# Attention in front of two expert layers: bias by sums in one small tile, ends of two sequences as 64-row products, transposes among products, weights later, products of zeros while k loads

## The chip, the core and the metric

The kernel runs on one core of one Trainium2 chip. Its engines are TensorE (PE), VectorE (DVE), ScalarE (ACT), GpSimd (POOL) and SyncE (SP, which issues every DMA of this kernel). The metric is the device time of one execution in microseconds (us); the time before is 2064.96 us, the median of three runs (2064.05 to 2070.14).

## What is computed

Three stages follow each other:

```python
# 1. attention with random features; q, k, v are (4, 8, 576, 64), omega is (128, 64)
q_s, k_s = q * scale, k * scale
def phi(x):
    h = einsum('bhsd,md->bhsm', x, omega) - sum(x * x, axis=-1) / 2
    return exp(h - max(h, axis=-1)) / sqrt(128)
kv, z = einsum('bhsm,bhsd->bhmd', phi(k_s), v), sum(phi(k_s), axis=2)
out = einsum('bhsm,bhmd->bhsd', phi(q_s), kv) / (einsum('bhsm,bhm->bhs', phi(q_s), z) + 1e-6)
# 2. eight experts on the 2304 tokens: gates by eight rounds of row and column sums,
#    out += gate[:, e] * (relu(x @ w1[e]) @ w2[e])
# 3. h = x @ w_in; g = h * sigmoid(1.702 h); g @ w_out
```

## The kernel before

Every step is recorded first. `Plan.add` takes an operation with its engine, an estimated duration and the tiles that it reads and writes; `Plan.run` then lists the operations engine by engine in the order in which a clock of its own would start them, and that order is written into the program. On the chip each engine works through its own list strictly in order and waits at the head of it for whatever that instruction needs. Operations of PE marked `main` keep the order in which they were recorded; the other engines take the operation with the earliest due time. `nb` is the earliest time at which the plan lets an operation start.

**Attention** goes by tiles of 128 tokens and 8 heads: 4 whole tiles for each of the 4 sequences, and one tile for the last 64 tokens of two sequences together (a tail). `attention()` builds a list of 36 steps (k tiles of a sequence, then its q tiles) and runs a pipeline over it. At step `s`:

- `squares` for tile `s+5`: POOL squares the tile (L529), DVE sums each head (L530) into `ss`.
- `project_in` for `s+4`: four PE transposes (L539), ACT and DVE split the result into a rounded part and a rest (L545, L548).
- `transpose_q` for a q tile `s`: eight PE transposes of its features (L642), ACT copies (L647).
- `features` for `s+2`: in two halves of four heads, six products each with omega (L566 to L568) into one PSUM bank each; DVE takes the maximum of each head (L574).
- `exps` for `s+2`: two small DVE operations on 128x8 (L590, L595) make the bias from `ss` and the maximum, then eight ACT exponentials (L602) read the two banks. The banks are six, taken in turn; a bank is free again when its reader is done.
- `kv_step` for a k tile (L615), or `attend` for a q tile (L659): eight products (each shown as two instructions) into the PSUM tile `pair`; for q, `divide` on DVE (L676, L681, L684).
- `transpose_x` for q tile `s-1`: four transposes (L698), ACT and DVE write the token block (L702, L705); after six tiles `x_operands` sums the pieces of the block on POOL (L405) and sends them to DRAM (`sx`).

For a q tail `attend` runs once with the first sequence's sums, `divide` writes 64 rows, then `attend` runs again with the other sequence's sums into the same `pair`, and `divide` writes the other 64 rows.

**The weights** of the first two products are recorded ahead of attention: `load_gate` (L470, L473) and `prepare(0, ...)` with `split`: four DMAs into `raw` for each half, four differences on POOL (L405, raw<-raw), then ACT casts (L1075) and POOL rests (L405, w1x and w2x).

**The expert layers** (`all_visits`) multiply by seven products of half blocks: L1169 up, L1314 down. `load_x` brings the seven pieces of a token block from `sx` into `xo`, seven DMAs of 768 KB, into room in which the attention stage kept omega and its split tiles. The first four products of the first visit are taken early, at the places of `EARLY` within the last steps of attention. The first product of all (L1387) only wipes a bank.

## Time and profile before

| what | value |
|---|---|
| median of three runs | 2064.96 us (2064.05 to 2070.14) |
| the profiled execution's own time, its span | 2075.01 us, 2073.2 us |
| mean granted TensorE clock in it | 0.984 of full speed |
| PE busy | 2007.5 us, 97% of the span |
| DVE, ACT, POOL busy | 1474.2 us (71%), 1080.6 us (52%), 1270.5 us (61%) |
| chain that ended last, by engine | PE 78%, DVE 13%, ACT 3%, DMA 2% |

"Busy" counts the time in which an engine has an instruction in it. PE counts as busy at either of its two clocks, 1.2 and 2.4 GHz, so a stretch in which PE is always busy can still take twice its time at full speed; the granted clock (PEclk) tells which. The idle time of an engine matters where the chain of waits passes through it.

### The profile page before, as it was taken

To read this page: it belongs to the slowest core of one execution; us is meant where nothing else is said; L and a number is where in the kernel's file an instruction comes from. 1 tells how busy PE (TensorE), PEld (TensorE's weight loads), DVE (VectorE), ACT (ScalarE), POOL (GpSimd) and SP (SyncE) were. 2 spreads that over 40 slices of the span, in tenths; PEclk is the share of its full clock that TensorE was granted. 3 is DMA by queue.
4 is the path that set the end of the run, shared out by engine and by line. 5 is a ranking of instruction groups with operands and counts; after the bars stand their busy time and mean duration, and the time that the engine had idled before them with its cause. 6 is when DMAs were issued, how large, how long until landed. Compare 5 with 4: busy or idle time off the path is not lost.

```text
span 2073.2 us, 39087 instructions
## 1 busy us (share of the span) xinstructions
PE 2007.5 (97%) x14191; PEld 1971.0 (95%) x14191; DVE 1474.2 (71%) x2965; ACT 1080.6 (52%) x2537; POOL 1270.5 (61%) x1215
## 2 busy tenths in 40 slices
PE   7999999999999999999999999999999889999998
PEld 7998999999999999999999999999999889999998
DVE  6876458877777767677777777776566687567666
ACT  5777564555344444544544354445435466745654
POOL 4475856667485665848666584766647265647453
PEclk8998999999999999999999999999999999999999
DMA  9554665566566656656765565665556798646553
GB/s 192 121 171 166 218 245 209 193 258 225 209 258 252 218 211 240 239 207 246 261 223 209 227 255 201 237 238 218 180 198 254 222 287 279 226 160 230 219 193 128
DMA packets 246898, 451.97 MB, mean 218 GB/s; under 512 B 73648, under 2 KB 186800, under 8 KB 246704
## 3 DMA queue, kind: packets, MB, share of 16 engines
q1 hardware_dynamic: 246704, 449.47, 61.5%
q8 instruction: 112, 1.84, 0.3%
q14 instruction: 82, 0.67, 0.1%
HBM read 403.26 MB, written 46.14 MB: 217 GB/s over the span
## 4 chain that ended last, share of the span: by engine, by line
PE 78%; DVE 13%; ACT 3%; DMA 2%; issue 1%; POOL 0%; SPq 0%; DVEq 0%; ACTq 0%; POOLq 0%
PE bank L1169 37%; PE bank L1314 35%; DVE ring L1201 2%; DVE h L405 2%; DMA sx<-x2s 2%; DVE acc L1347 1%; PE pair L659 1%; PE pair L615 1%; DVE bank L1190 1%; ACT acc L602 1%; ACT h L1179 1%; PE bank L566 1%; DVE h L1228 1%; DVE x2s L990 1%; PE bank L642 1%
## 5 line engine op out<-in xcount | busy, mean ns | idle before, releaser
L1314 PE MATMUL bank<-w2x,h 128*128 128x256 f32 x7560 | 939.3, 281 | 32.4 <-DVE acc L1347 12.8
L1314 PEld LDWEIGHTS bank<-w2x,h 128*128 128x128 f32 x7560 | 917.3, 189 | 47.5 <-DVE acc L1347 17.3
L1169 PE MATMUL bank<-xo,w1x 128*128 128x384 f32 x5040 | 919.7, 337 | 4.6 <-ACT ring L1179 3.8
L1169 PEld LDWEIGHTS bank<-xo,w1x 128*128 128x128 f32 x5040 | 869.8, 189 | 11.5 <-ACT ring L1179 9.7
L405 POOL TENSOR_TENSOR h<-ring,h 128x384 fp32r<-128x384 f32 x387 | 421.0, 1114 | 100.2 <-ACT h L1179 98.2
L1347 DVE SCALAR_TENSOR_TENSOR acc<-bank,sig,acc 128x256 f32<-128x256 f32 x756 | 328.2, 477 | 134.9 <-PE bank L1314 134.2
L405 POOL TENSOR_TENSOR w1x<-raw,w1x 128x768 fp32r<-128x768 f32 (+1 forms) x120 | 182.6, 1528 | 250.9 <-ACT w1x L1075 240.5
L405 POOL TENSOR_TENSOR raw<-raw 128x256 f32<-128x256 f32 x320 | 241.9, 781 | 100.4 <-DMA raw<-in_moe_w_dram 66.4
L1179 ACT ACTIVATE ring<-bank 128x384 f32<-128x384 f32 x480 | 233.2, 491 | 123.0 <-PE bank L1169 118.7
L1179 ACT ACTIVATE bank<-bank 128x384 f32<-128x384 f32 x120 | 57.0, 475 | 453.7 <-PE bank L1169 427.4
L1228 DVE SCALAR_TENSOR_TENSOR h<-bank,h 128x384 fp32r<-128x384 f32 x288 | 158.9, 554 | 172.4 <-ACT ring L1179 159.5
L1179 ACT ACTIVATE h<-ring 128x384 fp32r<-128x384 f32 x480 | 231.0, 528 | 71.4 <-DVE ring L1201 61.2
L405 POOL TENSOR_TENSOR w2x<-raw,w2x 128x768 fp32r<-128x768 f32 (+1 forms) x120 | 180.7, 1514 | 52.8 <-ACT w2x L1075 52.3
L1179 ACT ACTIVATE h<-bank 128x384 fp32r<-128x384 f32 x360 | 176.1, 494 | 69.6 <-DVE bank L1190 44.5
L1201 DVE SCALAR_TENSOR_TENSOR ring<-bank,ring 128x384 f32<-128x384 f32 x384 | 191.9, 547 | 21.6 <-PE bank L1169 21.6
L405 POOL TENSOR_TENSOR ring<-ring 128x384 f32<-128x384 f32 (+1 forms) x106 | 111.1, 1049 | 150.1 <-ACT ring L1179 138.8
L1190 DVE TENSOR_TENSOR bank<-bank,ring 128x384 f32<-128x384 f32 x240 | 133.6, 560 | 39.4 <-PE bank L1169 38.3
L1340 DVE TENSOR_TENSOR acc<-bank,acc 128x256 f32<-128x256 f32 x252 | 95.6, 418 | 59.2 <-PE bank L1314 58.3
L1075 ACT CAST w2x<-raw 128x768 fp32r<-128x768 f32 (+1 forms) x120 | 82.7, 696 | 91.9 <-POOL raw L405 91.9
L405 DVE TENSOR_TENSOR h<-ring,h 128x384 fp32r<-128x384 f32 x93 | 96.4, 1048 | 1.4 <-ACT h L1179 1.1
L1075 ACT CAST w1x<-raw 128x768 fp32r<-128x768 f32 (+1 forms) x120 | 82.7, 695 | 18.4 <-PE bank L1169 9.6
L602 ACT ACTIVATE acc<-bank,acc 128x128 f32<-128x128 f32 x272 | 77.0, 401 | 26.0 <-DVE acc L595 19.0
(127 smaller groups left out, 1503.7 us busy)
## 6 DMA issues: line engine op xcount, KB each, us to landing
xo<-sx SPq DMA_DIRECT2D x420, 768.0 KB, 6.9
raw<-in_moe_w_dram SPq DMA_DIRECT2D x256, 128.0 KB, 4.2
sx<-x2s SPq DMA_DIRECT2D x126, 128.0 KB, 4.4
x2s<-in_moe_w_in_dram SPq DMA_DIRECT2D x16, 512.0 KB, 5.2
x2s<-in_moe_w_out_dram SPq DMA_DIRECT2D x16, 512.0 KB, 8.7
sx<-ring SPq DMA_DIRECT2D x32, 192.0 KB, 3.1
b<-in_k_dram SPq DMA_DIRECT2D x16, 256.0 KB, 4.8
b<-in_v_dram SPq DMA_DIRECT2D x16, 256.0 KB, 4.4
```

The source lines that it names most:

```text
L405: lambda e: e.tensor_tensor(out=out(), in0=a(), in1=b(), op=op), r, w,
L566: nc.tensor.matmul(o, hi[:, u], om_hi, start=True, stop=False)
L602: lambda h=h, pv=pv: nc.scalar.activation(f[:, h, :], pv[:, h % 4, :], AF.Exp, bias=nb[:, h : h + 1]),
L1075: lambda e, a=a, b=b: nc.scalar.copy(T[w, c, 0][:, a:b], r[:, a:b]), raws, [(w, c, g, 0)],
L1169: nc.tensor.matmul(o(b), T["w1", c, a][:, slot, kk], T["xo"][x][:, y, kk], start=start and kk == 0 and n == 0, stop=kk == 1 and n == 2, sk ...
L1179: rec("ACT", act_us(Q), lambda e: nc.scalar.activation(out(), src(), f, **kw), r, w)
L1190: lambda e: e.tensor_tensor(out=out[0](), in0=a[0](), in1=b[0](), op=op), [a[1], b[1]], [out[1]],
L1201: lambda e: e.scalar_tensor_tensor(out=RT(out), in0=o(b), scalar=0.0, in1=RT(c), op0=ALU.max, op1=op),
L1228: lambda e: e.scalar_tensor_tensor(out=g(), in0=src[0](), scalar=0.0, in1=h().bitcast(F32), op0=ALU.max, op1=ALU.subtract),
L1314: nc.tensor.matmul(bank[i][:, u], T["h", c, a, x][:, t * P : (t + 1) * P], T["w2", c, y][:, slot], start=s and m == 0, stop=c == 1 and m = ...
L1340: lambda e, q=q, i=i, u=u: e.tensor_tensor(out=q, in0=bank[i][:, u], in1=q, op=ALU.add),
L1347: lambda e, q=q, i=i, u=u, g=g: e.scalar_tensor_tensor(out=q, in0=bank[i][:, u], scalar=g, in1=q, op0=ALU.mult, op1=ALU.add),
```

## The change

- The bias comes from sums within one small tile `four` of four sets of columns: `c * ss`, the negated maximum (the projections are negated, so a minimum), their sum, and `-c * ss`. Two `tensor_scalar` operations write the first and last set from `ss` in `squares`; in `exps` two `tensor_reduce` operations (L615, L619 of the new file) add neighbouring sets, where two `scalar_tensor_tensor` operations stood. The exponentials take scale -1.
- A q tail is attended once: per head two products of 64 columns of the transposed features, one for each sequence's sums, into rows 0 to 63 and 64 to 127 of `pair`; then one `divide` of 128 rows.
- `features`, `transpose_q`, `kv_step` and `attend` go by halves of four heads and are interleaved; `transpose_x` stands between the halves of `attend`, or of the first `kv_step` after a q tile.
- The gate, w1 and the first half of w2 are loaded no earlier than 40, 60 and 80 us of the plan, which also counts 4 or 5 us more for their landing; tiles of q, k and v count as longer transfers in the plan.
- Ten products with a tile of zeros, 384 columns each, stand on PE while the first k tiles load, and ten more at step 0, ahead of the features of tile 2. They go into `pair` and nothing reads them.
- `EARLY` names other places for the first four products of the first visit.

```diff
-                    o.end = bus + 1.9
+                    o.end = bus + 1.9 + o.lag
...
+    idle = XO[:, 0:Q]
...
+        nc.vector.memset(idle, 0.0)
...
-        dma(lambda: wg_raw, lambda: w_gate.rearrange("(k p) e -> p k e", p=P), (), ["wg_raw"], 0.02)
+        dma(lambda: wg_raw, lambda: w_gate.rearrange("(k p) e -> p k e", p=P), (), ["wg_raw"], 0.02, nb=60.0, lag=5.0)
...
+    def products_of_zeros(n):
+        z = idle.bitcast(F32R)
+
+        def fn():
+            for _ in range(n):
+                nc.tensor.matmul(PAIR[:, 0, :Q], z[:, 0:P], z, start=True, stop=True, skip_group_check=True)
+
+        pe(n * MM, fn, [("xo", 0)], [PAIRS[0]])
...
-        sums[what, b, t] = ss, k
+        four, kf = little("four")
+        c = 0.5 * SCALE * SCALE
+        for a, y in ((0, c), (3, -c)):
+            dve(
+                0.16,
+                lambda a=a, y=y: nc.vector.tensor_scalar(
+                    out=four[:, a * H : (a + 1) * H], in0=ss, scalar1=y, scalar2=None, op0=ALU.mult
+                ),
+                [k], [kf + (a,)],
+            )
+        sums[what, b, t] = four, kf
...
-                    out=mx[:, 4 * half : 4 * half + 4], in_=pv, op=ALU.max, axis=AX.X
+                    out=four[:, H + 4 * half : H + 4 * half + 4], in_=pv, op=ALU.min, axis=AX.X
...
+        def pair(a):
+            return four[:, a * H : (a + 2) * H].rearrange("p (a h) -> p h a", a=2)
+
         dve(
-            0.26,
-            lambda: V.scalar_tensor_tensor(out=hm, in0=ss, scalar=c, in1=mx, op0=ALU.mult, op1=ALU.add),
-            [ks, km], [kh],
+            0.18,
+            lambda: V.tensor_reduce(out=four[:, 2 * H : 3 * H], in_=pair(0), op=ALU.add, axis=AX.X),
+            [k4 + (0,), k4 + (1,)], [k4 + (2,)],
         )
         dve(
-            0.26,
-            lambda: V.scalar_tensor_tensor(out=nb, in0=ss, scalar=c, in1=hm, op0=ALU.mult, op1=ALU.subtract),
-            [ks, kh], [kn],
+            0.18, lambda: V.tensor_reduce(out=nb, in_=pair(2), op=ALU.add, axis=AX.X),
+            [k4 + (2,), k4 + (3,)], [kn],
         )
...
-    def attend(ft, b):
-        (ft, kf), (kx, kk) = ft, kvs[b]
+    def attend(ft, b, t):
+
+        ft, kf = ft
+        parts = ((slice(0, P), kvs[b]),) if t < NT else tuple(
+            (slice(i * TAIL, (i + 1) * TAIL), kvs[b - 1 + i]) for i in range(2)
+        )
 
-        def fn():
-            for h in range(H):
-                nc.tensor.matmul(
-                    PAIR[:, h // 4, (h % 4) * VW : (h % 4) * VW + D + 1], ft[:, h, :], kx[:, h, 0 : D + 1],
-                    start=True, stop=True,
-                )
+        def fn(half):
+            for h in range(4 * half, 4 * half + 4):
+                for r, (kx, _) in parts:
+                    nc.tensor.matmul(
+                        PAIR[r, h // 4, (h % 4) * VW : (h % 4) * VW + D + 1], ft[:, h, r], kx[:, h, 0 : D + 1],
+                        start=True, stop=True, skip_group_check=True,
+                    )
...
+            if s == -5:
+                products_of_zeros(10)
...
+            if s == 0:
+                products_of_zeros(10)
+            pvs = next(pj, None)
+            if what == "q":
+                ft = next(tq)
+            elif steps and at(s - 1, "k"):
+                next(steps[0])
+            next(pj, None)
...
+            if what == "q":
+                next(tq)
+                yield s - n, 0
+                steps = [attend(ft, b, t)]
+            if steps:
+                next(steps[0])
+            if at(s + 2, "kq"):
+                exps(pvs, four, f2)
+            if at(s - 1, "q"):
+                transpose_x(xs.pop(s - 1), *column(s - 1))
+            for x in steps:
+                take(x, 3)
...
-    EARLY = ((-1, 1), (-1, 3), (0, 1), (0, 3))
+    EARLY = ((-2, 0), (-2, 1), (-1, 0), (-1, 1))
...
-            prepare(0, "w1", c, 0)
+            prepare(0, "w1", c, 0, nb=40.0 + 20.0 * c, lag=4.0)
             split("w1", c, 0)
-        prepare(0, "w2", 0, 0)
+        prepare(0, "w2", 0, 0, nb=80.0, lag=4.0)
```

The order of the instructions moves at three places of which the prediction speaks.

POOL in the first q tiles, where the differences of the first weights stand among the squares; `raw<-raw` are the differences, which wait for the weights' DMAs, and `acc<-b` the squares. Before:

```order
L529 TENSOR_TENSOR acc_73<-b_96 128x512
L529 TENSOR_TENSOR acc_73<-b_97 128x512
L529 TENSOR_TENSOR acc_73<-b_98 128x512
L501 MEMSET b_94 128x8
L529 TENSOR_TENSOR acc_73<-b_80 128x512
L405 TENSOR_TENSOR raw_67<-raw_67 128x256 x4
L529 TENSOR_TENSOR acc_73<-b_82 128x512
L405 TENSOR_TENSOR w1x<-raw_67,w1x 128x512
```

Now:

```order
L541 TENSOR_TENSOR acc_73<-b_86 128x512
L541 TENSOR_TENSOR acc_73<-b_88 128x512
L541 TENSOR_TENSOR acc_73<-b_89 128x512
L513 MEMSET b_98 128x8
L541 TENSOR_TENSOR raw_68<-b_84 128x512
L541 TENSOR_TENSOR acc_73<-b_90 128x512
L513 MEMSET b_80 128x8
L541 TENSOR_TENSOR acc_73<-b_87 128x512
L407 TENSOR_TENSOR raw_67<-raw_67 128x256
L541 TENSOR_TENSOR acc_73<-b_91 128x512
L407 TENSOR_TENSOR raw_67<-raw_67 128x256
```

The differences moved behind seven more squares, and squares stand between them.

PE in a step of a whole q tile (`xo` are the features' operands, `acc` the features to transpose in L642 or L670; L698 and L735 are `transpose_x`, L539 `project_in`). Before, from the last product of a tile's features to the first of the next:

```order
L568 MATMUL bank_103<-xo 128x256
L659 MATMUL pair<-raw_68,acc_72 128x65 x8
L698 MATMUL bank_104<-ident,raw_68 128x128 x4
L539 MATMUL bank_105<-ident,b_97 128x128 x4
L642 MATMUL bank_100<-ident,acc_73 128x128 x4
L642 MATMUL bank_101<-ident,acc_73 128x128 x4
L566 MATMUL bank_102<-xo 128x256
```

Now, from the last product of the first half's features to the second half of `attend`:

```order
L590 MATMUL bank_100<-xo 128x256
L670 MATMUL bank_101<-ident,acc_72 128x128 x4
L588 MATMUL bank_102<-xo 128x256
L589 MATMUL bank_102<-xo 128x256
L590 MATMUL bank_102<-xo 128x256
L588 MATMUL bank_102<-xo 128x256
L589 MATMUL bank_102<-xo 128x256
L590 MATMUL bank_102<-xo 128x256
L670 MATMUL bank_103<-ident,acc_72 128x128 x4
L692 MATMUL pair<-raw_68,acc_72 128x65 x4
L735 MATMUL bank_104<-ident,raw_68 128x128 x4
L692 MATMUL pair<-raw_68,acc_72 128x65 x4
```

The transposes of the features now stand between and behind the halves of the features, and `transpose_x` stands between the halves of `attend`.

PE at the end of attention, from the last product of the last features (L568, L590) on; L1387 and L1438 wipe a bank, L1169 and L1220 are the first visit's products. Before:

```order
L568 MATMUL bank_104<-xo 128x256
L659 MATMUL pair<-raw_68,acc_72 128x65 x8
L698 MATMUL bank_105<-ident,acc_73 128x128 x4
L642 MATMUL bank_104<-ident,acc_73 128x128 x4
L642 MATMUL bank_105<-ident,acc_73 128x128 x4
L659 MATMUL pair<-raw_68,acc_72 128x65 x8
L698 MATMUL bank_104<-ident,raw_68 128x128 x4
L642 MATMUL bank_105<-ident,acc_72 128x128 x4
L642 MATMUL bank_104<-ident,acc_72 128x128 x4
L659 MATMUL pair<-raw_68,acc_73 128x65 x8
L1387 MATMUL bank_102<-xo,w1x 128x384
L1169 MATMUL bank_100<-xo,w1x 128x384 x6
```

Now:

```order
L590 MATMUL bank_103<-xo 128x256
L670 MATMUL bank_104<-ident,acc_72 128x128 x4
L692 MATMUL pair<-raw_68,acc_72 128x65 x4
L735 MATMUL bank_105<-ident,acc_73 128x128 x4
L692 MATMUL pair<-raw_68,acc_72 128x65 x4
L670 MATMUL bank_104<-ident,acc_73 128x128 x4
L670 MATMUL bank_105<-ident,acc_73 128x128 x4
L1438 MATMUL bank_102<-xo,w1x 128x384
L1220 MATMUL bank_100<-xo,w1x 128x384 x6
L692 MATMUL pair<-raw_68,acc_72 128x65 x4
L735 MATMUL bank_104<-ident,raw_68 128x128 x4
L692 MATMUL pair<-raw_68,acc_72 128x65 x4
```

The transposes of the last q tile but one take banks 104 and 105; before, 104 was one of the two banks of the last features, and now these are 101 and 103. The wipe and the first product moved ahead of two attends.

## Rows read from the trace of the kernel before

**Rows 1.** Windows of core 0, attention by its k and q phases, then the rest: length, busy us (instructions) of each engine, granted clock, DMA

```profile
7.43:35.83 28.40, 26.39 (x193) 25.75 (x193) 24.41 (x49) 17.41 (x56) 12.69 (x16) 0.88 1.21 217
35.83:67.37 31.54, 25.06 (x173) 23.86 (x173) 18.09 (x37) 19.62 (x54) 13.39 (x17) 0.84 0.51 115
67.37:87.00 19.63, 17.62 (x150) 16.91 (x149) 18.40 (x32) 13.58 (x44) 12.80 (x15) 1.00 0.83 206
87.00:141.64 54.64, 50.97 (x398) 49.52 (x397) 39.99 (x81) 36.90 (x110) 34.26 (x39) 0.91 0.49 146
141.64:179.29 37.65, 37.11 (x321) 36.16 (x320) 29.74 (x64) 31.82 (x96) 21.09 (x22) 1.00 0.28 95
179.29:219.66 40.37, 37.22 (x228) 35.78 (x228) 18.29 (x36) 22.93 (x58) 21.22 (x22) 0.75 0.64 223
219.66:2073.16 1853.50, 1810.45 (x12728) 1781.41 (x12726) 1322.84 (x2664) 935.83 (x2118) 1151.93 (x1074) 0.99 0.62 225
```

**Rows 2.** Windows again, the stretches of attention at half clock

```profile
15.55:22.37 6.82, 6.82 (x33) 6.82 (x34) 5.74 (x10) 3.35 (x12) 2.88 (x3) 0.50 1.30 217
42.86:53.10 10.24, 9.43 (x44) 9.43 (x45) 5.93 (x12) 7.89 (x23) 4.10 (x5) 0.50 0.54 120
87.23:90.64 3.41, 3.41 (x18) 3.41 (x17) 0.69 (x1) 2.53 (x6) 0.27 (x2) 0.50 0.57 127
117.95:124.77 6.82, 6.82 (x33) 6.82 (x34) 3.19 (x7) 1.73 (x5) 4.27 (x5) 0.50 0.33 101
...
196.46:213.52 17.06, 15.77 (x67) 15.05 (x68) 4.28 (x10) 6.85 (x16) 4.86 (x5) 0.50 0.86 313
```

**Rows 3.** Timeline of PE: start, us, line, tiles [idle before <-releaser]

```profile
14.36 0.38 PE L566 MATMUL bank<-xo 128*128 128x256 f32 x1 [1.95 <-ACT acc L602]
...
43.67 0.58 PE L566 MATMUL bank<-xo 128*128 128x256 f32 x1 [5.61 <-ACT acc L602]
...
117.86 3.62 PE L659 MATMUL pair<-raw,acc 128*128 128x65 f32 x16 [2.95 <-DVE raw L684]
...
197.21 1.97 PE L642 MATMUL bank<-ident,acc 128*128 128x128 f32 x8 [2.48 <-ACT acc L602]
```

**Rows 4.** Timeline of POOL and DVE at the second of these waits

```profile
40.40 2.21 POOL L405 TENSOR_TENSOR raw<-raw 128x256 f32<-128x256 f32 x3 [6.64 <-DMA raw<-in_moe_w_dram]
...
44.10 0.38 DVE L473 TENSOR_TENSOR acc<-acc 128x16 f32<-128x16 f32 x1 [7.73 <-DMA acc<-in_moe_w_gate_dram]
```

**Rows 5.** Chain that ended last, one later piece of six wide products

```profile
232.97 1.04 PE bank L1169 x6
```

**Rows 6.** Timeline of PE, features behind transposes

```profile
130.88 0.36 PE L566 MATMUL bank<-xo 128*128 128x256 f32 x1
131.08 0.28 PE L567 MATMUL bank<-xo 128*128 128x256 f32 x1
131.19 0.28 PE L568 MATMUL bank<-xo 128*128 128x256 f32 x1
```

**Rows 7.** Lines of 0 to 220 us by form: busy us, mean ns | idle before

```profile
L590 DVE SCALAR_TENSOR_TENSOR acc<-acc 128x8 f32<-128x8 f32 x36 | 14.4, 400 | 0.6
...
L615 PE MATMUL pair<-b,acc 128*128 128x65 f32 x256 | 32.1, 281 | 1.6 <-DVE acc L684 1.6
...
L615 PE MATMUL pair<-b,ring 64*128 64x65 f32 x64 | 8.0, 275 | 0.0
```

**Rows 8.** Timeline, a small operation of DVE beside a square on POOL

```profile
12.07 1.04 POOL L529 TENSOR_TENSOR acc<-b 128x512 f32<-128x512 f32 x1 [0.99 <-DVE acc L590]
12.49 0.64 DVE L595 SCALAR_TENSOR_TENSOR acc<-acc 128x8 f32<-128x8 f32 x1
```

**Rows 9.** Two lines of the expert stage: durations in ns, min/median/max

```profile
L858 DVE TENSOR_SCALAR sig<-sig x8: 161/338/787, 307.7 to 385.6; 128x18 f32<-128x18 f32 x8
...
L857 DVE TENSOR_REDUCE sig<-sig x8: 286/290/305, 307.3 to 385.0; 128x18 f32<-128x144 f32 x8
```

**Rows 10.** DMA issues of 186 to 215 us: count, KB each, median us to landing

```profile
xo<-sx SPq DMA_DIRECT2D x5, 768.0 KB, 8.0
```

147 lines of the change are left out of this document (72 added, 75 removed).

## The prediction

> **What bounds the kernel now.** I read the windows first [rows 1]. From 219.66 us on PE is busy 1810.45 of 1853.50 us; there the change records the same products in the same order, so I look for nothing there. Attention before it is another matter: six stretches from 7.43 to 219.66 us, 212.2 us in all, in which PE idles 2.01 + 6.48 + 2.01 + 3.67 + 0.54 + 3.15 = 17.9 us and the granted clock is as low as 0.75. Next, the stretches at half clock [rows 2]: the five shown hold 6.82, 9.43, 3.41, 6.82 and 15.77 us of busy PE at the lower of its two levels (1.2 instead of 2.4 GHz), and one more of 3.41 us lies at 179.39 us. What PE did in them takes half the time at full clock, so they cost 45.7 / 2 = 22.8 us. Idle and clock together are 40.7 us, about a fifth of attention and 2% of the kernel. That is all that this change can win.
>
> Then, what stood before each slow stretch. Four of the six begin inside a wait of PE or within 1.2 us of its end [rows 3]: 1.95 us for an exponential, until 14.36; 5.61 us for one, until 43.67; 2.95 us for the division of a q tail, until 117.86; 2.48 us for an exponential, until 197.21. The other two, at 87.23 and 179.39 us, follow no wait: there the program has two `kv_step`s in a row, 32 instructions of 65 columns. So a wait costs more than itself here, since the clock falls behind it.
>
> What ended the long waits is in the timeline of the other engines [rows 4]: POOL stood 6.64 us at the first difference of w1, whose DMA had not landed, with the squares of later tiles queued behind it, and DVE stood 7.73 us at L473, whose gate had not landed, with the maxima and biases queued behind. PE's 5.61 us are these two heads of queues.
>
> **The change part by part**, against the profiled execution of 2075.01 us (span 2073.2 us). That run is 10 us above the median of 2064.96 us, so I subtract the sum from the median.
>
> *Weights later.* It removes the 5.61 us and, if no new wait takes their place, the slow stretch behind them, 9.43 / 2 = 4.7 us: 10.3 us. Ends: 5.6 (the clock falls anyway) and 11.2 (all idle of that q phase, 6.48 us, too). I take 10.3. What covers it: by POOL's order seven more squares go ahead of the first difference, and the squares that come behind it belong to tiles whose features are many steps away. What is late next is the x operands at the end, below.
>
> *Zeros.* The first ten stand where PE waits for k; they cost nothing unless they outlast the load. A product of 384 columns takes 1.04 / 6 = 0.17 us [rows 5], so the second ten take 1.74 us, in a place where PE waited 1.95 us [rows 3]. That is 0.2 us won by itself, and 6.82 / 2 = 3.4 us if the clock then holds: 3.6 us, with 0.2 as the low end. If the shorter bias had ended that wait early, zeros would cost up to what they fill, 1.7 us.
>
> *Bias.* Ahead of the exponentials stood two operations of 400 ns mean [rows 7]; an undisturbed one takes about 0.16, as the minimum of a small tensor_scalar shows [rows 9], and the reductions now in their place were not stretched anywhere (286 to 305 ns for 18 results of 144 inputs [rows 9]). The chain from the last maximum to the first exponential gets shorter by 0.2 to 0.5 us per tile. That is worth something only where PE waits for an exponential or a division; I count 1.0 us for the third stretch of the windows, of its 2.01 us of idle, ends 0 and 2.0. DVE's own work hardly changes: 36 tiles lose two operations of 0.40 us and gain four of 0.16 to 0.29 us.
>
> *Ends of two sequences.* The 2.95 us at 117.86 are the second `attend` of a q tail waiting for the first `divide`. With one `attend` of 32 products and one `divide` that wait has no place any more, and neither has the slow stretch behind it, 6.82 / 2 = 3.4 us: 6.4 us, ends 2.95 and 8.8 (everything lost from 87 to 141.64). PE's work stays: 32 instructions before and now. Do the 64-row products cost less? Products that use half the array are in the trace, the k tails: 275 ns mean against 281 for whole ones [rows 7]. I count no gain. The Trainium skill (TensorEngine Tiling (Array Packing), Key Properties) says that different tiles of the array can run in parallel; the new products alternate between the two column halves, and by that page the two tails together would lose half of 64 instructions of 1.73 / 16 = 0.11 us, 3.5 us. The same section says that a change of tiling mode drains the engine, which would take some of that back. No row here shows either, and the sum goes by the rows.
>
> *Transposes among products, other early places.* At the end the last q tile but one no longer transposes into a bank of the last features, so the 2.48 us wait goes, and with it, if nothing else makes PE wait, most of the 15.77 / 2 = 7.9 us. Late next are the x operands: omega's room is free only after the last features, and five loads of 768 KB then queue on SP with 8.0 us median to landing [rows 10]. Between the last features and the third product of the visit PE now has 28 transposes (eight took 1.97 us at half clock [rows 3], so 3.4 us), two `attend`s (3.62 at half clock [rows 3], so 3.6 us) and two products (2.1 us [rows 5]), 9 us in all; two loads stand ahead of the one that the third product needs, so it may wait 0 to 3 us; I take 1.5, and 0.4 for small ones: 2.5 + 7.9 - 1.9 = 8.5 us, ends 0 and 12. Against that, features follow products of another kind once more per tile, and the first of them starts its successor 0.20 us later instead of 0.11 [rows 6]: 34 tiles x 0.09 = 3 us lost, ends 0 and 6.
>
> *Half clock after the k tails.* 1.7 us each, twice. The new order still has 24 instructions in a row there instead of 32; I take them as unchanged.
>
> **Sum:** 10.3 + 3.6 + 1.0 + 6.4 + 8.5 - 3 = 26.8, say 27 us. From the median: 2064.96 - 27 = **2038 us**. With all low ends: 5.6 + 0.2 + 0 + 3.0 + 0 - 6 = 2.8, 2062; with all high ends 11.2 + 3.6 + 2.0 + 8.8 + 12 - 0 = 37.6, 2027.
>
> **The rivals.**
>
> *The clock does not come back.* The waits go and the slow stretches stay. For it: two of six slow stretches had no wait before them [rows 2], only dense products of 65 columns. Against it: the four long ones each follow a wait. It gives 0.2 + 5.6 + 1.0 + 2.95 + 1.0 - 3 = 7.8 us, 2057.
>
> *The x operands become the last wait.* The early products now come up to three attends sooner, and the loads do not, since they wait for the last features. If PE waits 4 us there instead of 1.5, the clock falls again as behind the other waits and the 7.9 us are not won: 26.8 - 7.9 - 2.5 = 16.4, 2048.
>
> *DVE behind POOL (slower).* A small operation of DVE with its data in SBUF waits for POOL: L595 beside a square took 0.64 us and ended with it, at 13.1 [rows 8], and the tensor_scalar L858 ranges from 161 to 787 ns, while the reduction L857 stays at 290 [rows 9]. The Trainium skill (SBUF — State Buffer, Who interferes with whom) names the same: tensor_scalar can lock the port pair that DVE shares with GpSimd, tensor_reduce never does on this chip; these rows agree. The change puts two such tensor_scalar operations per tile into DVE's list right behind a square's sum, where the next square is often running. DVE is busy 24.41 + 18.09 + 18.40 + 39.99 + 29.74 + 18.29 = 148.9 us in attention [rows 1]; less 72 x 0.40, plus 144 x 0.17, it is 144.6. If each of the 72 waited w, PE would be held up as soon as 144.6 + 72 w passes the 185 us that I forecast for the stage, at w = 0.57; at a whole square, 1.04 us, DVE needs 219.5 us against the 212.2 of before: 2072. The median of L858 stands for w = 0.18, far below.
>
> That the change does not do what it says I exclude: the orders above show each part.
>
> **How the numbers follow.** About 0.3% (6 us) is what a measurement of this kernel can tell from no change. Forecast, 2030 to 2047, with all four long waits gone: 0.60. Clock stays low, 2057: 0.13. X operands last, 2048: 0.14. Two of these together, or part of the DVE rival, within 6 us of before: 0.08. DVE behind POOL, 2072: 0.05. Faster is 0.60 + 0.13 + 0.14 = 0.87, same 0.08, slower 0.05. The range reaches from 2027 (all high ends) to 2058 (the clock's rival) and leaves out the last two cases and little below.
>
> **What would show it.** Weights: no idle of PE above 2 us between 36 and 60 us, and no wait of POOL for `raw` longer than about 1 us with a square behind it. Zeros: PEclk 1.00 from 15 to 23 us. Ends: no wait of PE for the division near the q tails, and one group of DVE divisions per tail. End: the transposes of the last q tile but one without a wait, PEclk 1.00 in the last 20 us of attention, and the first gate products some 27 us earlier than 219.66. Bias: tensor_scalar with a maximum near 1 us, the two reductions flat. The prediction is wrong if the gate products come earlier and the end does not, or if slow stretches follow no wait.

## The result and the profile after

The changed kernel takes 2040.85 us in the median (2035.49 to 2043.02), the kernel before beside it 2066.77 us (2064.05 to 2070.14): ratio 0.9873, 95% interval 0.9855 to 0.9891. 2038 was forecast; of the 27 us forecast as won, 25.9 came. The profiled execution took 2040.57 us (span 2038.8 us, mean granted clock 0.995), close to its median; that of before had taken 2075.01 us, 8 us above its own. Between the two traces 34.4 us therefore have to be found, and which part of attention the profiled run of before lost beyond its neighbours can't be seen.

The windows of the kernel after, by the phases of [rows 1] (same first instant, then each phase to the end of its last `kv_step` or `attend`; columns as there):

```profile
7.43:35.28 27.85, 25.50 (x204) 23.96 (x203) 26.63 (x71) 17.48 (x57) 13.46 (x16) 1.00 1.28 214
35.28:55.45 20.17, 19.73 (x174) 19.27 (x174) 16.57 (x46) 17.41 (x49) 4.99 (x7) 1.00 0.77 160
55.45:72.92 17.47, 17.04 (x150) 16.66 (x149) 15.97 (x41) 13.69 (x44) 12.44 (x15) 1.00 0.86 221
72.92:122.05 49.13, 45.73 (x397) 43.81 (x396) 41.88 (x100) 38.40 (x113) 36.64 (x42) 0.97 0.55 158
122.05:160.11 38.06, 37.31 (x322) 36.05 (x321) 30.16 (x75) 33.32 (x99) 26.28 (x28) 1.00 0.37 130
160.11:188.95 28.84, 26.08 (x228) 24.63 (x228) 13.77 (x34) 21.57 (x57) 17.65 (x20) 1.00 0.69 246
188.95:2038.80 1849.85, 1808.88 (x12728) 1779.84 (x12726) 1319.23 (x2672) 936.25 (x2119) 1143.70 (x1069) 1.00 0.63 226
```

Against [rows 1] the six phases of attention changed by -0.55, -11.37, -2.16, -5.51, +0.41 and -11.53 us, 30.7 us in all, and the rest by -3.65 us. The first gate product, the mark between the two, starts at 188.95 us instead of 219.66. Six stretches at half clock became one, the last of these three lines. The first two are the k tails; behind them the kernel before lost the clock without any wait [rows 2], and the changed kernel keeps it:

```profile
70.21:73.00 2.79, 2.79 (x25) 2.65 (x25) 2.65 (x6) 2.07 (x7) 2.79 (x3) 1.00 0.75 168
157.41:160.20 2.79, 2.79 (x25) 2.65 (x25) 1.54 (x4) 1.82 (x7) 2.63 (x3) 1.00 0.46 170
105.16:108.57 3.41, 3.41 (x19) 3.41 (x18) 2.00 (x4) 2.86 (x10) 3.41 (x4) 0.50 0.71 263
```

The timeline of PE, its waits of over 0.8 us after the first 4 us; where [rows 3] had 1.95, 5.61, 2.95 and 2.48 us, it now has:

```profile
16.64 0.38 PE L588 MATMUL bank<-xo 128*128 128x256 f32 x1 [1.44 <-ACT acc L626]
...
103.22 1.08 PE L641 MATMUL pair<-b,acc 128*128 128x65 f32 x8 [2.56 <-POOL acc L541]
...
182.23 1.28 PE L1220 MATMUL bank<-xo,w1x 128*128 128x384 f32 x6 [1.52 <-DMA xo<-sx]
...
187.40 0.66 PE L735 MATMUL bank<-ident,acc 128*128 128x128 f32 x4 [0.82 <-DVE acc L721]
```

The wait at 103.22 us is new. It stands at the first `kv_step` behind the first q tail, which needs the tail's `divide` (L713 to L721). The view names a square on POOL, but the division ends at 103.12 us, 0.1 us before PE goes on. DVE and POOL there, in the timeline:

```profile
97.61 1.33 DVE L548 TENSOR_SCALAR acc<-acc 128x8 f32<-128x8 f32 x2
99.04 0.69 DVE L542 TENSOR_REDUCE acc<-acc 128x8 f32<-128x512 f32 x1
99.94 0.69 DVE L542 TENSOR_REDUCE acc<-acc 128x8 f32<-128x512 f32 x1 [0.21 <-POOL acc L541]
100.55 0.16 DVE L713 TENSOR_SCALAR acc<-pair 128x8 f32<-128x8 f32 x1
100.66 1.20 DVE L548 TENSOR_SCALAR acc<-acc 128x8 f32<-128x8 f32 x2
...
102.44 0.68 DVE L721 TENSOR_TENSOR raw<-pair,acc 128x512 f32<-128x512 f32 x1
```

```profile
95.99 1.96 POOL L407 TENSOR_TENSOR ring<-ring,xo 128x384 f32<-128x384 f32 x2
97.91 1.00 POOL L407 TENSOR_TENSOR ring<-ring,w2x 128x384 f32<-128x384 f32 x1
98.87 1.04 POOL L541 TENSOR_TENSOR acc<-b 128x512 f32<-128x512 f32 x1
```

POOL is busy without a gap with the sums of `x_operands` (L407 on `ring`); squares stand between them, the sums of these squares (L542) stand ahead of the division on DVE, and the `tensor_scalar` operations (L548) stretch. Only 0.21 us there is a wait of DVE for a square; the two pairs of `tensor_scalar` take 2.53 us. `x_operands` is due after six finished tiles and meets the first q tail here.

### The profile page after: what moved, and what is told of

The parts are those of the page before. It is cut to its first block, busy times and chain, and to the rows that moved or that the text cites. A ratio compares the mean times of both kernels' runs of the same rounds, so it can differ in the third digit from the quotient of the medians.

```text
span 2038.8 us, 39158 instructions
## 1 busy us (share of the span) xinstructions
PE 1984.5 (97%) x14211; PEld 1948.2 (96%) x14211; DVE 1466.4 (72%) x3040; ACT 1080.3 (53%) x2537; POOL 1257.5 (62%) x1207
## 4 chain that ended last, share of the span: by engine, by line
PE 81%; DVE 11%; DMA 3%; ACT 3%; issue 1%; POOL 1%; SPq 0%; DVEq 0%; ACTq 0%; POOLq 0%
PE bank L1220 38%; PE bank L1365 37%; DVE h L407 2%; DVE ring L1252 2%; PE pair L641 2%; DVE acc L1398 1%; DVE bank L1241 1%; DVE x2s L1041 1%; ACT h L1230 1%; PE bank L588 1%; DMA sx<-x2s 1%; DMA sx<-acc 1%; PE bank L589 1%; PE pair L692 1%; PE bank L590 1%
## 5 line engine op out<-in xcount | busy, mean ns | idle before, releaser
L1365 PE MATMUL bank<-w2x,h 128*128 128x256 f32 x7560 | 940.1, 281 | 33.4 <-DVE acc L1398 11.8
L1220 PE MATMUL bank<-xo,w1x 128*128 128x384 f32 x5040 | 915.9, 336 | 3.7 <-ACT ring L1230 1.6
L1220 PEld LDWEIGHTS bank<-xo,w1x 128*128 128x128 f32 x5040 | 866.7, 188 | 10.2 <-ACT ring L1230 6.3
L407 POOL TENSOR_TENSOR h<-ring,h 128x384 fp32r<-128x384 f32 x382 | 413.4, 1107 | 96.2 <-ACT h L1230 93.7
L407 POOL TENSOR_TENSOR w1x<-raw,w1x 128x768 fp32r<-128x768 f32 (+1 forms) x120 | 181.3, 1520 | 265.2 <-ACT w1x L1126 256.3
L407 POOL TENSOR_TENSOR raw<-raw 128x256 f32<-128x256 f32 x320 | 240.7, 777 | 83.8 <-DMA raw<-in_moe_w_dram 55.0
L407 POOL TENSOR_TENSOR w2x<-raw,w2x 128x768 fp32r<-128x768 f32 (+1 forms) x120 | 180.9, 1515 | 54.9 <-ACT w2x L1126 54.5
L407 POOL TENSOR_TENSOR ring<-ring 128x384 f32<-128x384 f32 (+1 forms) x106 | 112.2, 1059 | 155.4 <-ACT ring L1230 143.6
L407 DVE TENSOR_TENSOR h<-ring,h 128x384 fp32r<-128x384 f32 x98 | 99.6, 1027 | 1.3 <-ACT h L1230 1.0
```

What stands on the lines that cost most here:

```text
L407: lambda e: e.tensor_tensor(out=out(), in0=a(), in1=b(), op=op), r, w,
L1220: nc.tensor.matmul(o(b), T["w1", c, a][:, slot, kk], T["xo"][x][:, y, kk], start=start and kk == 0 and n == 0, stop=kk == 1 and n == 2, sk ...
L1365: nc.tensor.matmul(bank[i][:, u], T["h", c, a, x][:, t * P : (t + 1) * P], T["w2", c, y][:, slot], start=s and m == 0, stop=c == 1 and m = ...
```

## The experiments

For all fourteen profiles, core 0 up to the first gate product: PE's idle time, what the clock cost (half of PE's busy time in the stretches at the granted clock 0.50) and the remainder, called work. Each of these comes from one execution: in the six profiles in which PE's list is the same up to there, the features of tile 2 start between 16.64 and 17.52 us, so differences of about 1 us between two rows tell nothing. Times are medians of four runs. The kernels were timed on several chips, so ratios to the kernel before on the same chip are compared.

| kernel | median us | ratio (95%) | first gate product | idle | clock | work | after it |
|---|---|---|---|---|---|---|---|
| before | 2066.77 | 1 | 219.66 | 22.6 | 22.8 | 174.2 | 1853.5 |
| changed | 2040.85 | 0.9873 (0.9855 to 0.9891) | 188.95 | 13.3 | 1.7 | 173.9 | 1849.9 |
| a1 weights early | 2039.03 | 0.9872 (0.9841 to 0.9903) | 192.10 | 12.5 | 5.1 | 174.4 | 1846.3 |
| a5 plan costs too | 2050.41 | 0.9903 (0.9884 to 0.9922) | 198.05 | 20.4 | 4.3 | 173.3 | 1851.8 |
| a2 no second zeros | 2044.66 | 0.9896 (0.9871 to 0.9922) | 193.72 | 15.8 | 6.3 | 171.6 | 1849.6 |
| a4 halves apart | 2038.84 | 0.9873 (0.9847 to 0.9898) | 190.43 | 12.2 | 3.1 | 175.1 | 1847.8 |
| b2 tail twice | 2052.10 | 0.9919 (0.9892 to 0.9946) | 196.34 | 14.1 | 4.3 | 177.9 | 1852.5 |
| b5 not interleaved | 2041.30 | 0.9867 (0.9845 to 0.9889) | 195.10 | 11.8 | 10.2 | 173.1 | 1846.7 |
| b3 late products | 2044.87 | 0.9891 (0.9859 to 0.9922) | 193.55 | 12.3 | 6.8 | 174.4 | 1851.3 |
| b1 old bias | 2036.78 | 0.9845 (0.9828 to 0.9862) | 188.80 | 12.1 | 1.7 | 175.0 | 1845.5 |
| b6 scale on ACT | 2040.21 | 0.9867 (0.9840 to 0.9895) | 189.06 | 11.5 | 3.3 | 174.3 | 1848.5 |
| b4 no squares | 2024.53 | 0.9804 (0.9779 to 0.9829) | 178.24 | 7.2 | 0.0 | 171.0 | 1844.1 |
| c1 and no second zeros | 2030.56 | 0.9822 (0.9795 to 0.9849) | 181.31 | 9.5 | 1.7 | 170.1 | 1846.4 |
| c2 and no zeros | 2030.73 | 0.9825 (0.9799 to 0.9850) | 180.65 | 10.4 | 1.7 | 168.6 | 1848.5 |

The last column varies from 1844 to 1853 us though its products are the same, so the first gate product tells the effects in attention better than the time does. Between the changed kernel and its variants only differences of some 6 us stand out in the time.

### Weights later

```diff
-            prepare(0, "w1", c, 0, nb=40.0 + 20.0 * c, lag=4.0)
+            prepare(0, "w1", c, 0)
```

and the same for the gate and w2 (run a1). In a5, besides, the transfer of a tile in the plan:

```diff
-                [kx], [kx], 0.45,
+                [kx], [kx], 0.262,
```

> The changed kernel with one part undone: the gate, w1 and the first half of w2 are loaded as early as before (no earliest times of 40, 60 and 80 us, no added landing time in the plan). My theory, a wait costs itself and the half clock behind it: the differences of w1 stand at the head of POOL's list again and the gate's at DVE's, PE idles for about 5 us in one wait for an exponential between 36 and 60 us, a stretch of 3.4 to 9.4 us at the granted clock 0.50 follows, the first gate product comes at 197 to 200 us instead of 188.95, and the time is about 2051 us. Rival, the new order alone bears it (shorter bias, transposes among products): the longest wait there stays under 2 us, the first gate product comes before 192 us, the time stays within 3 us of 2041.

> The changed kernel with the weights loaded as early as before and, beyond the run with only that, the transfer of a tile of q, k or v counted in the plan as before (0.262 instead of 0.45). Only now does the first difference of w1 stand on POOL ahead of seven squares again, and the gate early on DVE's list; with the earliest times alone removed it stood where the change has it. My theory, the wait of 5.61 us was POOL's and DVE's heads of queue: PE idles 4 to 6 us in one wait for an exponential between 36 and 60 us, half clock behind it, first gate product 8 to 12 us later than the 188.95 of the changed kernel, time about 2050 us. Rival, the loads land early enough in the new order (zeros, shorter bias, transposes among products leave more slack): no wait above 2 us there, first gate product within 3 us of 189 to 192, time within 3 us of 2041.

In a1 nothing came back: its first difference starts at 60.75 us, in the changed kernel at 60.48. Its 3.15 us are a half-clock stretch behind the wait at 17 us (below). In a5 the weights are early again, PE's wait is longer than expected, and the first gate product comes 9.1 us later. The timelines of POOL, DVE, ACT and PE:

```profile
40.74 0.72 POOL L407 TENSOR_TENSOR raw<-raw 128x256 f32<-128x256 f32 x1 [7.73 <-DMA raw<-in_moe_w_dram]
```

```profile
44.37 0.60 DVE L476 TENSOR_TENSOR acc<-acc 128x16 f32<-128x16 f32 x1 [8.55 <-DMA acc<-in_moe_w_gate_dram]
```

```profile
45.17 1.14 ACT L626 ACTIVATE acc<-bank,acc 128x128 f32<-128x128 f32 x4 [2.85 <-DVE acc L619]
```

```profile
46.37 1.12 PE L670 MATMUL bank<-ident,acc 128*128 128x128 f32 x4 [9.97 <-ACT acc L626]
```

So heads of queues that wait for weights were the cause, as predicted, but the one that lets go last differs. In a5 it is DVE's: the bias of the tile (L619) stands behind the gate's first operation, and the exponentials and PE behind the bias. In the kernel before it was ACT's, where a cast of w1 stood 7.49 us for POOL's differences, with the exponentials behind it:

```profile
41.96 0.62 ACT L1075 CAST w1x<-raw 128x512 fp32r<-128x512 f32 x1 [7.49 <-POOL raw L405]
```

No square is in either chain. The 9.1 us are a net figure: the wait of 9.97 us and the clock's 4.3 us are more, and a5 waits less elsewhere (0.94 us at the first q tail). The larger charge for the tiles' transfers is enough to keep the wait away: with it the plan expects the weights later by itself. The earliest times, which I had taken for the cause, matter little where that charge stands; whether they would be enough without it, no run shows.

### Zeros

```diff
-            if s == 0:
-                products_of_zeros(10)
```

> The changed kernel without its second ten products of zeros (those ahead of the features of tile 2). My theory: PE waits there for the exponentials for about 3.2 us instead of 1.44 us, until the same 16.6 us; the clock falls to 0.50 for 6.82 us behind that wait, which costs 3.4 us; first gate product at about 192.4 us, time about 2044 us. Rival, the zeros do nothing for the clock (their place in the order of the other engines and the shorter bias made it hold): granted clock 1.00 from 15 to 25 us, first gate product within 0.7 us of 188.95.

First gate product 193.72 us, 4.8 us later, where my theory had 3.4:

```profile
16.88 0.43 PE L588 MATMUL bank<-xo 128*128 128x256 f32 x1 [2.47 <-ACT acc L626]
```

The clock falls behind this wait, but for 3.42 us only, which costs 1.7; the products from 20 to 82 us come 1.5 us later than in the changed kernel, and that is what the second ten are worth at their place. The other 3.3 us come later: a wait of 1.15 us at 91, a half-clock stretch twice as long behind the wait at 106, and one more at 191. Why these came, no run tells. So my theory holds in direction; its size came out by other waits. Nor is it a rule. In five variants PE's list is the same up to 17 us as in the changed kernel, zeros included, and PE waits there as long. In two (a4, b2) the clock held, as in the changed kernel; in a1, b3 and b5 it fell for about 7 us and cost 3.4. b3's timeline of PE, and its windows behind it:

```profile
17.52 0.39 PE L588 MATMUL bank<-xo 128*128 128x256 f32 x1 [1.47 <-ACT acc L626]
```

```profile
18.00:20.00 2.00, 1.93 (x14) 1.73 (x13) 2.00 (x6) 2.00 (x9) 1.77 (x2) 0.79 1.25 183
20.00:22.00 2.00, 2.00 (x12) 2.00 (x11) 2.00 (x9) 0.56 (x3) 0.39 (x2) 0.50 1.37 214
```

The same wait of 1.4 us was thus followed by half clock or not, and nothing in the rows tells which.

### Ends of two sequences

Run a4 changes only the order of the 64-column products, b2 attends a tail twice and divides 64 rows twice, as before.

```diff
-            for h in range(4 * half, 4 * half + 4):
-                for r, (kx, _) in parts:
+            for r, (kx, _) in parts:
+                for h in range(4 * half, 4 * half + 4):
```

```diff
-                steps = [attend(ft, b, t)]
+                steps = [attend(ft, b, t, 0 if t == NT else None)]
...
+            if what == "q" and t == NT:
+                take(attend(ft, b, t, 1), 3)
+                divide(x, slice(TAIL, 2 * TAIL))
```

> The changed kernel with the 64-column products of a q tail in another order: per half of attend first the four heads of rows 0 to 63, then the four of rows 64 to 127, where they alternated head by head. Same products, same count. In the changed kernel 16 such instructions take 0.62 us from their first start to the next group's, against 0.84 us for 8 whole ones. If the two column halves run side by side because neighbours lie in different halves, a group of 16 now takes 1.1 to 1.7 us, four groups cost 2 to 4 us, first gate product at about 191 to 193 us. If a 64-column product is just shorter by itself (0.62 / 16 = 0.039 us each in any order), a group still takes about 0.62 us and nothing moves.

> The changed kernel with a q tail attended twice as before: all eight heads with the first sequence's sums, a division of 64 rows, then all eight heads with the other's into the same tile and the other 64 rows. My theory: per tail a wait of PE for the first division of 2 to 3 us, and 32 instructions of 128 columns (1.7 us and more at full clock) in place of 1.24 us; half clock of 3.4 to 6.8 us behind the wait of the first tail. The second tail is at the end, where a product of the first visit stands next to it. Together first gate product 6 to 10 us later, at 195 to 199 us, time about 2049 us. Rival, the wait moves only (the changed kernel already waits 2.56 us for the division at 103.22): first gate product 2 to 4 us later, time about 2044 us.

The timeline of PE at the first q tail, changed kernel first, then a4:

```profile
95.80 0.60 PE L670 MATMUL bank<-ident,acc 128*128 128x128 f32 x4
96.33 0.69 PE L692 MATMUL pair<-raw,acc 128*64 128x65 f32 x16
96.95 0.66 PE L735 MATMUL bank<-ident,acc 128*128 128x128 f32 x4
```

```profile
97.19 0.97 PE L692 MATMUL pair<-raw,acc 128*64 128x65 f32 x16
98.08 0.66 PE L735 MATMUL bank<-ident,acc 128*128 128x128 f32 x4
```

Sixteen instructions of 64 columns take 0.62 us to the start of the next group where neighbours lie in different halves, and 0.89 us where they follow each other in one half. Eight whole ones take 0.84 us (172.86 to 173.70 us). So both expectations were half right: a 64-column product takes about half the time in either order, and alternating saves another 0.27 us per group. The lines of PE's weight loads in the changed kernel, by form, go the same way:

```profile
L692 PEld LDWEIGHTS pair<-raw,acc 128*128 128x128 f32 x256 | 31.1, 192 | 0.2
...
L641 PEld LDWEIGHTS pair<-b,ring 64*128 64x128 f32 x64 | 7.6, 187 | 0.7
...
L692 PEld LDWEIGHTS pair<-raw,acc 128*64 128x64 f32 x64 | 2.2, 137 | 0.8 <-issue 0.6 <-ACT ring L990 0.2
```

A load of 64 columns takes 137 ns, one of 64 rows 187, a whole one 192. The Trainium skill (TensorE: Matmul & The Clock Gate, LDWEIGHTS (loading the stationary operand)) states that a load takes time by its columns and not by its rows; these rows agree in direction, though 137 ns are more than half of 192. That the loads set the time of the products is argued from this, not shown. From the other page of the Trainium skill that the prediction named (TensorEngine Tiling (Array Packing), Key Properties) came an estimate of 3.5 us for two tails, where I took nothing; measured are 4.0 us of work in b2, 3.3 of them after 24 us. For the drain that this page names, there is little room: the four transposes ahead of a group of 64 columns take 0.53 us to its start (95.80 to 96.33), where 0.11 us each would make 0.44.

In b2 the second `attend` waits again, and the first gate product comes 7.4 us later, as my theory had it; its work is 4.0 us more, for the most part the products':

```profile
102.42 3.67 PE L694 MATMUL pair<-raw,acc 128*128 128x65 f32 x16 [3.21 <-DVE raw L724]
```

### Order of the products

Run b5 puts the transposes of the features ahead of them, `attend` whole, `transpose_x` behind it. Run b3 takes the first visit's products later.

```diff
-            pvs = next(pj, None)
             if what == "q":
                 ft = next(tq)
-            elif steps and at(s - 1, "k"):
-                next(steps[0])
+                next(tq)
+            pvs = next(pj, None)
             next(pj, None)
```

```diff
-    EARLY = ((-2, 0), (-2, 1), (-1, 0), (-1, 1))
+    EARLY = ((-1, 1), (0, 1), (1, 1), (2, 1))
```

> The changed kernel with PE's order in a step as before: both groups of transposes of a q tile's features, then the twelve products of the features, then all of attend or of the first kv_step, then transpose_x; places of the early products kept. My theory: at the end the transposes of the last tiles follow each other, PE waits for banks and divisions there by 2 to 4 us, with half clock behind; on the other side the features are entered from another kind of product once less per tile, 3 us less. First gate product at 188 to 194 us, time 2040 to 2046 us. Rival, the interleaving is what hides the exponentials and divisions in all of attention: waits of PE in each step, first gate product beyond 198 us, time beyond 2050 us.

> The changed kernel with the first four products of the first visit taken as late as before: the first behind the attend of the last q tile, the others behind the steps that follow, so that three attends stand next to each other at the end of attention again. My theory: the loads of the x operands are then no wait any more (1.52 us in the changed kernel), but PE waits for the divisions and transposes of the last three tiles by 2 to 5 us, with half clock behind it; first gate product at 191 to 195 us, time 2042 to 2047 us. Rival, the places don't matter, since the same products only change places with attends and what is left to wait for is DVE's division either way: first gate product within 1 us of 188.95.

b5 idles no more than the changed kernel, its work is 0.8 us less, but the clock costs it 10.2 us instead of 1.7; its first gate product comes 6.15 us later, 1.1 us beyond my theory's range. Of that 3.4 us are the stretch at 18 us; the one behind the wait for the first q tail's division is longer than in the changed kernel by 1.7; two more, of 1.7 us each, stand at the first k tail and at the end, where its last transposes wait 2.33 us. The windows of b5 at the first k tail, and its timeline of PE at the second and at the end:

```profile
72.52:76.27 3.75, 3.75 (x35) 3.61 (x33) 3.58 (x8) 2.54 (x10) 3.75 (x4) 1.00 0.72 153
76.37:79.78 3.41, 3.41 (x18) 3.41 (x19) 1.69 (x4) 2.91 (x8) 1.30 (x3) 0.53 0.85 206
```

```profile
162.04 1.90 PE L641 MATMUL pair<-b,acc 128*128 128x65 f32 x16
163.87 2.00 PE L641 MATMUL pair<-b,ring 64*128 64x65 f32 x16
...
181.81 1.50 PE L670 MATMUL bank<-ident,acc 128*128 128x128 f32 x8 [2.33 <-ACT acc L626]
```

With 32 products of 65 columns in a row, 72.52 to 76.27 us without a wait, the clock falls again behind the first k tail. Behind the second, with the same 32 from 162.04 us on, it holds, so this order can bring the stretch back but need not; with 24, and features between the others, the clock held behind both. In time b5 equals the changed kernel, since 3.1 us come back after the first gate product; why, no run tells.

In b3 the load of the x operands is no wait any more, as expected; but neither is it in the other variants that keep the squares, so the places don't show as the reason. The other waits of its end add up to no more than in the changed kernel, and the clock holds from 120 us on. Its 4.6 us are the stretch at 18 us (3.4) and a longer one behind the wait at 107; the end itself is 0.8 us shorter. The rival was right: alone, the places of the early products don't matter here.

Alone, the order does not matter much at the end either. From the last `kv_step` to the first gate product b5 takes 29.2 us and b3 28.0, the changed kernel 28.8 and the kernel before 40.3. The wait of [rows 3] at 197 us is back in b5 (2.33 us against 2.48), but half clock behind it costs 1.7 us instead of 7.9. A run with both undone is missing.

### Bias, squares, DVE and POOL

Run b1 has the old bias (two `scalar_tensor_tensor` in `exps`, no `tensor_scalar` in `squares`), b6 lets ACT write the two scaled sums, b4 has no squares at all, c1 and c2 are b4 without the second and without all zeros.

```diff
-            dve(
-                0.16,
-                lambda a=a, y=y: nc.vector.tensor_scalar(
-                    out=four[:, a * H : (a + 1) * H], in0=ss, scalar1=y, scalar2=None, op0=ALU.mult
-                ),
+            act(
+                0.2,
+                lambda a=a, y=y: nc.scalar.activation(four[:, a * H : (a + 1) * H], ss, AF.Copy, scale=y),
```

```diff
-        nb, kn = little("nb")
...
+        nb, kn = four[:, H : 2 * H], k4 + (1,)
```

b1's edit in `exps` (its second operation is the same with `nb` and `hm`; `ss`, which is now read later, has six buffers instead of two), and that of c2 beside the one of a2:

```diff
-            lambda: V.tensor_reduce(out=four[:, 2 * H : 3 * H], in_=pair(0), op=ALU.add, axis=AX.X),
+            lambda: V.scalar_tensor_tensor(out=hm, in0=ss, scalar=-c, in1=mn, op0=ALU.mult, op1=ALU.subtract),
```

```diff
-            if s == -5:
-                products_of_zeros(10)
```

> The changed kernel with the bias of before: no tensor_scalar behind the sums, two scalar_tensor_tensor operations on 128x8 ahead of the exponentials in place of the two reductions. My theory: the two operations stretch behind POOL as in the kernel before (400 ns mean against 167), the chain from the last minimum to the first exponential gets longer by 0.2 to 0.5 us per tile, PE waits for exponentials 1 to 3 us more in sum, time 2041 to 2045 us. Rival, the tensor_scalar operations at the head of DVE's list (302 ns mean, up to 0.9 us beside a square) cost as much as they save: first gate product within 1 us of 188.95 or up to 2 us earlier, since four operations per tile become two.

> The changed kernel with the 72 small operations that write c * ss and -c * ss moved from DVE to ACT (a copy with a scale); squares and sums stay. It takes away only the tensor_scalar operations that stretch beside POOL, where the run without squares took away the whole chain and came 10.7 us earlier to the first gate product. My theory, DVE behind POOL is the larger part of the remaining waits: the two pairs of 1.06 us at 8.3 and 10.5 us and those of 1.33 and 1.20 us at 97.6 and 100.7 us leave DVE's list, the waits of 1.44 us until 16.64 and of 2.56 us until 103.22 shrink to under 1 us each, and the half clock behind the latter goes: first gate product at 183 to 186 us, time about 2037 us. Rival, the squares and sums themselves (POOL's 1.04 and DVE's 0.69 us per tile) are what the chain waits for, and ACT, 76% busy there, now delays exponentials by 72 x 0.2 us: first gate product between 188 and 194 us.

> The changed kernel without the squares: POOL's 36 squares, DVE's 36 sums, the 72 tensor_scalar operations and the 72 small sums of the bias are left out, and the exponentials take the negated maximum itself as their bias (the sum of squares is added and taken away again in the bias, so it cancels but for rounding). It takes away the lock between DVE and POOL on the chain to the first features and at the q tail. If the remaining waits of attention hang on that chain (tensor_scalar behind POOL at 8.3, 10.5, 97.6 and 100.7 us; PE idle 1.44 us until 16.64 and 2.56 us until 103.22, half clock 3.41 us behind the latter): first gate product 4 to 7 us earlier, at 182 to 185 us, time about 2036 us. Rival, PE's own list is what bounds attention now: under 2 us earlier, within 2 us of 2041.

> The run without squares, and without the second ten products of zeros. In the run without squares PE never waited between 3 and 95 us, so the second ten have nothing left to fill. My theory: they cost their 1.7 to 2.0 us there; first gate product at about 176.3 us instead of 178.24, granted clock 1.00 from 15 to 25 us, time about 2022.5 us. Rival, without them PE waits for the first exponentials and the clock falls as in the run without them alone: first gate product at 178 us or later, time 2024 to 2028 us.

> As the run without squares and second zeros, and without the first ten as well. My theory: k's transposes then start when k lands, at about 5.0 us instead of 6.4, but at the price of half clock as in the kernel before (12 in 3.54 us against 1.65), so that the first features start at 8.2 us against 7.85: 0.3 us later by then, and nothing else changes; first gate product within 0.7 us of the run that keeps the first ten. Rival, the clock comes up later without them and the first features run at half clock too: 1 to 2 us later. Other rival, the zeros only outlast the load: 1 us earlier.

b1: first gate product at 188.80 us, 0.15 earlier. Its two operations are as slow as in [rows 7], by its lines of DVE:

```profile
L605 DVE SCALAR_TENSOR_TENSOR acc<-acc 128x8 f32<-128x8 f32 x36 | 16.3, 453 | 0.8
L610 DVE SCALAR_TENSOR_TENSOR acc<-acc 128x8 f32<-128x8 f32 x36 | 15.9, 441 | 0.9
```

The new reductions take 164 and 170 ns in the median and 173 at most, but the new `tensor_scalar` operations reach 1301 ns, and the features of tile 2 start at 16.64 us in the changed kernel and at 15.42 in b1. The wait for the first tail's division is gone in b1, and others for exponentials came (1.54 us until 93.94, with half clock behind it, 1.25 until 123.55, 1.15 until 143.52). The stretching only moved to another place of the chain. The rival was right; whether b1 is faster in time, as the intervals hint, they don't settle.

b6: 189.06 us, no gain, and the wait behind the q tail stays at 2.35 us. In its timelines of DVE and POOL the head of the queue is a sum that waits for its square:

```profile
101.01 0.69 DVE L542 TENSOR_REDUCE acc<-acc 128x8 f32<-128x512 f32 x1 [3.00 <-POOL acc L541]
101.61 0.15 DVE L711 TENSOR_SCALAR acc<-pair 128x8 f32<-128x8 f32 x1
```

```profile
98.97 1.00 POOL L407 TENSOR_TENSOR ring<-w2x,ring 128x384 f32<-128x384 f32 x1
99.93 1.04 POOL L541 TENSOR_TENSOR acc<-b 128x512 f32<-128x512 f32 x1
```

My theory fell: without the `tensor_scalar` operations on DVE the division waits as long, now for the square behind POOL's sums of the x operands. In the changed kernel DVE waited 0.21 us for a square at that place; moving the operations also made the plan order POOL's list anew, so b6 does not tell which of the two the 2.56 us were.

b4 removes that chain whole, and goes beyond the expectation: 178.24 us, 10.7 earlier, no half clock in attention at all, idle 7.2 us, and 2024.53 us (ratio 0.9804). 3.3 of the 10.7 us are won before 24 us and 3.3 at the first q tail, where 1.25 us of wait are left; the rest comes in small steps. It is the best version here, well under both kernels; the squares and their scaled sums are not needed, since the bias adds and subtracts the same sum.

c1 did not win the 2 us expected. The second ten products of zeros are gone and its work is smaller, but its first features start 1.7 us later than b4's (9.52 against 7.84 us), and from 17 to 168 us both are level. Then the timeline of PE reads, b4 first,

```profile
171.77 1.28 PE L1193 MATMUL bank<-xo,w1x 128*128 128x384 f32 x6 [1.37 <-DMA xo<-sx]
```

```profile
173.38 2.26 PE L1191 MATMUL bank<-xo,w1x 128*128 128x384 f32 x6 [2.93 <-DMA xo<-sx]
```

and in c1 the clock falls behind this wait for 3.4 us. That is the prediction's second rival, the x operands as the last wait; the rival of the expectation, a wait for the first exponentials, did not come. Attention ahead of it was no shorter than in b4: the load that PE waits for landed 1.6 us later, and why, no run tells. c2 starts its first features at 8.26 us (9.52 in c1, which had its first DMA 0.5 us later), and its gate product is 0.66 us earlier: the first ten zeros bring nothing. In the twelve profiles with them the first features start between 7.84 and 9.52 us, without them at 8.20 (before) and 8.26.

## Why the prediction was right, point by point

- **What bounds the kernel** held: idle and half clock in attention fell from 45.4 to 15.0 us up to the first gate product (table), 30.4 of the 30.7 us; work fell by 0.3, since before 24 us it rose by 3.7, the products of zeros among it, and behind that it fell by 4.0.
- **Weights later**, 10.3 us: the phase of 35 us won 11.4, and a5 gave back 9.1 net. Right in size, and right that heads of queues hold PE up. ACT's, which let go last in the kernel before, I had missed, and which edit moves the differences I had wrong.
- **Zeros**, 3.6 us: too much. The half clock of [rows 2] went (3.4), but tile 2's features start 2.3 us later than before, at 16.64 instead of 14.36, of which b1, with the old bias, gives back 1.2; the first phase won 0.55. The step that failed is that this wait would only be filled. And the first ten, which I let cost nothing unless they outlast the load, did outlast it: k's first transposes start at 6.44 us instead of 5.01.
- **Bias**, 1.0 us: nothing. I had priced the `tensor_scalar` operations at their undisturbed 0.16 us; they took 302 ns in the mean and up to 1301. The phase from 55 us did win 2.2 us, but no run here brings its wait back, so what won it stays open.
- **Ends of two sequences**, 6.4 us: undoing it costs 7.4. That the size is near is luck, from two errors that cancel. 64-column products save about 2.1 us per tail (4 groups of 0.84 us against 2 of 0.62), where I took nothing; the row I went by, products of 64 rows, was not the nearest. And the division's wait came back in another place with its half clock, 2.56 + 1.7 us.
- **End of attention**, 8.5 us: the last phase won 11.5, of which 1.7 belong to a k tail and 2.1 to the 64-column products: 7.7. Which edit did this stays open: the order alone (b5) and the early places alone (b3) hardly give anything back, and both undone were not run. The wait for the x operands was put at 1.5 and is 1.52 us, by luck: in the nine variants that keep the squares there is none.
- **Features entered once more per tile**, -3 us: work in b5 is 0.8 us less, or 1.3 if counted from the same `kv_step` at about 25 us, so the term is less than half of what I took. I had read only that the first product's successor starts 0.20 us after it [rows 6]; but the first itself starts close behind the transposes. In the changed kernel four transposes and the first product take 0.56 us together, no more than five times 0.11:

```profile
74.11 0.60 PE L670 MATMUL bank<-ident,acc 128*128 128x128 f32 x4
74.46 0.36 PE L588 MATMUL bank<-xo 128*128 128x256 f32 x1
74.67 0.28 PE L589 MATMUL bank<-xo 128*128 128x256 f32 x1
```

- **Half clock behind the k tails**, taken as unchanged: both are gone, 3.4 us, and b5 brings one of the two back.

The terms were read from a profiled execution 10 us above the median of before, and against that execution the changed kernel won 30.7 us in attention, not 27. So 25.9 us between the medians lie nearer to the forecast than the terms do: zeros, bias and the cost of entering features were too high, the 64-column products and the k tails were left out.

The rival of the clock was wrong as a whole, though at 17 us it is a matter of chance. "DVE behind POOL" as a slower kernel did not come, but its place did: of the two waits left by DVE, at 16.64 and 103.22 us, b4 removes one and halves the other.

## What to carry to other kernels

Where a wait is followed by half clock, price the wait with its stretch, and look which instruction stands at the head of the late engine's queue, on every engine of the chain: here consumers of a late DMA on POOL, ACT and DVE cost some 10 us. Before speeding up a small operation, ask whether the value is needed; the squares, which cancel, were worth 10.7 us up to the first gate product and some 14 to 16 in the time, more than any one part that was undone. Undo parts one by one and, where neither of two gives the gain back, both together. After each gain look for what was hidden: the x operands, no wait in the kernel before, took 1.4 to 3.0 us in four of the later profiles.

## What the runs showed of the hardware

A wait of 1.44 to 1.47 us at the same place of the same list was followed by half clock in three of six profiles. A stretch with no wait at all, 32 products of 65 columns in 3.75 us, was followed by it too in three of four places (both k tails of the kernel before, one of two in b5), and 24 of them at the two k tails of the changed kernel were not. A weight load takes 192 ns for 128 columns, 187 for 64 rows of 128 columns, 137 for 64 columns; eight products with whole weights take 0.84 us, sixteen with 64 columns 0.89, and 0.62 where neighbours lie in different column halves.
